# A linear-attention kernel whose first K-weight block is loaded and multiplied as two halves of 256 columns

## The chip, the cores and the metric

One core of one Trainium2 chip runs the whole program. The metric is the device time in microseconds of one execution. A change is judged by the medians of several executions of the kernel before and after it.

The engines are named as the profile names them: PE is TensorE (matmuls and transposes), PEld its weight loads, DVE is VectorE, ACT is ScalarE, POOL is GpSimd, and SPq is the queue of SyncE, which here only issues DMAs.

## The reference: what is computed

The input x has 2048 rows of 1024 bf16 numbers. Branch `a` is a linear attention with 32 heads of 32; branch `b` adds a gated feed-forward result to the single row that a router picks; a sigmoid gate mixes the two.

```python
qkv = x @ wqkv                               # 1024 -> 3 x 1024, split into heads
phi = lambda t: where(t > 0, t + 1, exp(t)) + 1e-6
pq, pk = phi(q), phi(k)
kv = einsum("bhsd,bhse->bhde", pk, v)        # summed over all 2048 rows
z  = einsum("bhsd->bhd", pk)
a  = (pq @ kv) / (pq @ z + 1e-6) @ wo
b  = x + (row argmax(x @ w_r): sigmoid * swiglu(x_sel) @ w_down)
out = g * a + (1 - g) * b                    # g = sigmoid(x . gate_w)
```

## The kernel before

**Tiling.** The 2048 rows are 16 tiles `t` of 128 rows (P = 128). The 1024 input features are 8 chunks `c` (KC = 8). TensorE contracts over partitions, so x must be on chip transposed: `xT[:, c, rows]`. For tiles 4 to 15 a transposing DMA writes `xT` (lines 134 and 135). For tiles 0 to 3 x is loaded as it is (`load_x`, lines 114 to 118), TensorE transposes it, and DVE (tiles 0 to 2) or ACT (tile 3) copies the result out of PSUM: `unit_T`, lines 196 to 206. One `unit_T` is eight 128x128 transposes and one copy of 128x1024.

**K and V.** `wkv` holds the K and V weights, 2048 columns in four blocks `nb` of 512. For a row tile and a block, `kv_mm` (lines 217 to 220) issues eight matmuls of 128x512, one for each chunk, into one PSUM bank. For K (nb 0 and 1), `phi_exp` on ACT takes the exponential and `phi_dve` on DVE two more operations (lines 183 to 191); for V, ACT copies.

**The opening.** The order on SP is written out in lines 126 to 136: row tile 0, the first quarter of the first weight block (`load_w0`: two chunks, 512 columns each), row tile 1, the other three quarters, row tiles 2 and 3 in one DMA, the three other blocks of `wkv`, three transposing DMAs, then the Q weights. The order on PE is written out in lines 253 to 274:

- seven matmuls on zeros (`warm(N_WARM)`), the transposes of tile 0, three more on zeros;
- two chunks of tile 0's K block, the transposes of tile 1, two chunks, one matmul on zeros, the last four chunks;
- four chunks of tile 1's block, the transposes of tile 2, the last four chunks of tile 1;
- the transposes of tile 3, then the blocks of tiles 2 and 3 (lines 273 and 274).

Line 283 then transposes the router weights (`wps` in the profile), and lines 285 to 287 run blocks 1 to 3 of tiles 0 to 3. After that the tiles go on one by one, with Q units and the feed-forward pieces set among them, and the output stage ends the program.

**What fixes the order.** The wrapper `in_order` (lines 68 to 81) ties each instruction of PE, DVE, ACT and SP to the one issued before it on the same engine, as long as `strict[0]` is true; it is so until line 290. Up to there each engine runs its instructions exactly as written. PSUM tiles with the tag "w" share four banks (`ps_work`, line 60): the results of the transposes and those of the matmuls both.

**In the profile.** The recorded line of every wrapped instruction is the wrapper's, L73, so groups are told apart by tile names: `warm_ps` is a matmul on zeros, `pst` a transpose of x, `ps<-wkv,xT` a K or V matmul, `xT<-pst` the copy behind a transpose, `xnat` the loaded row tiles.

Of the kernel before, what the change touches and what calls it, by code (L numbers as in the profile page):

```python
# [12 lines left out]
F32 = mybir.dt.float32  # L13
# [7 lines left out]
P = 128  # L21
S = 2048
D = 1024
F = 3584
NT = S // P
KC = D // P
NG = D // P
EPS = 1e-6
N_WARM = 7
Q_PER_T = {4: 2, 5: 1, 6: 1, 7: 2, 8: 1, 9: 1, 10: 2, 11: 1, 12: 1, 13: 2, 14: 1, 15: 0}  # L30
FFN_PER_T = {6: 8, 7: 0, 8: 8, 9: 0, 10: 8, 11: 0, 12: 8, 13: 1, 14: 7, 15: 7}
FFN_DEPTH = 10
# [4 lines left out]
def kernel(  # L37
# [16 lines left out]
    wqkv_v = A_wqkv.rearrange("(c p) n -> p c n", p=P)  # L54
# [5 lines left out]
    ps_work = ctx.enter_context(tc.tile_pool(name="ps_work", bufs=4, space=PSUM))  # L60
# [7 lines left out]
    def in_order(engine, names):  # L68
        last = [None]

        def wrap(fn):
            def call(*a, **k):
                inst = fn(*a, **k)  # L73
                if last[0] is not None and strict[0]:
                    tc.add_manual_dep(inst.ins, last[0].ins.name, NOSYNC, reason="program order on this engine")
                last[0] = inst
                return inst

            return call

        return SimpleNamespace(**{n: wrap(getattr(engine, n)) for n in names})

    pe = in_order(nc.tensor, ["matmul", "transpose"])
    dve = in_order(nc.vector, ["memset", "tensor_copy", "tensor_scalar", "tensor_scalar_add", "tensor_tensor", "scalar_tensor_tensor",
                               "reciprocal", "max", "max_index", "tensor_reduce", "stream_shuffle"])
    sp = in_order(nc.sync, ["dma_start", "dma_start_transpose"])
# [12 lines left out]
    xT = pa.tile([P, KC, S], BF)  # L99
# [7 lines left out]
    wkv = pw.tile([P, KC, 2 * D], BF)  # L107
# [6 lines left out]
    def load_x(t0, n):  # L114
        xt4 = xin.tile([P, n, D], BF, name=f"xnat{t0}", bufs=1)
        sp.dma_start(out=xt4[:, 0:n, :], in_=x_v[:, t0 : t0 + n, :])
        for i in range(n):
            xnat[t0 + i] = xt4[:, i, :]

    def load_w0(c2):  # L120
        sp.dma_start(out=wkv[:, 2 * c2 : 2 * c2 + 2, 0:512], in_=wqkv_v[:, 2 * c2 : 2 * c2 + 2, D : D + 512])

    def load_wkv(nb):
        sp.dma_start(out=wkv[:, :, 512 * nb : 512 * nb + 512], in_=wqkv_v[:, :, D + 512 * nb : D + 512 * nb + 512])

    load_x(0, 1)
    load_w0(0)
    load_x(1, 1)
    for c2 in range(1, 4):
        load_w0(c2)  # L130
    load_x(2, 2)
    for nb in range(1, 4):
        load_wkv(nb)
    for g4 in range(1, 4):
# [48 lines left out]
    def phi_exp(ps):  # L183
        e0 = tmp.tile([P, 512], F32, tag="phi_e0")
        act.activation(e0[:], ps, ACTF.Exp)
        return e0

    def phi_dve(ps, e0, out_ap):
        e1 = tmp.tile([P, 512], F32, tag="phi_e1")
        dve.tensor_scalar(e1[:], e0[:], 1.0, EPS, op0=ALU.min, op1=ALU.add)  # L190
        dve.scalar_tensor_tensor(out_ap, ps, 0.0, e1[:], op0=ALU.max, op1=ALU.add)
# [4 lines left out]
    def unit_T(t):  # L196
        xt = xnat[t]
        pst = ps_work.tile([P, D], BF, tag="w")
        for c in range(KC):
            pe.transpose(pst[:, c * P : (c + 1) * P], xt[:, c * P : (c + 1) * P], ident[:])  # L200
        dst = xT[:, :, t * P : (t + 1) * P]
        src = pst[:].rearrange("p (c s) -> p c s", c=KC)
        if t < 3:
            dve.tensor_copy(dst, src)
        else:
            act.copy(dst, src)

    pk_t = {}
    vt_t = {}

    def kv_open(t):
        if t not in pk_t:
            pk_t[t] = kvp.tile([P, D], BF, tag="pk", name=f"pk{t}")
            vt_t[t] = kvp.tile([P, NG, 129], BF, tag="vt", name=f"vt{t}")
            nc.gpsimd.memset(vt_t[t][:, :, 128:129], 1.0)  # L215

    def kv_mm(ps, t, nb, c0, c1):
        for c in range(c0, c1):
            pe.matmul(ps[:], lhsT=xT[:, c, t * P : (t + 1) * P], rhs=wkv[:, c, 512 * nb : 512 * nb + 512],
                             start=(c == 0), stop=(c == KC - 1))  # L220

    def kv_evac(ps, t, nb):
        if nb < 2:
            phi_dve(ps[:], phi_exp(ps[:]), pk_t[t][:, 512 * nb : 512 * nb + 512])
        else:
            act.copy(vt_t[t][:, 4 * (nb - 2) : 4 * (nb - 2) + 4, 0:128], ps[:].rearrange("p (g e) -> p g e", g=4))

    def unit_KV(t, nb):
        kv_open(t)
        ps = ps_work.tile([P, 512], F32, tag="w")  # L230
        kv_mm(ps, t, nb, 0, KC)
        kv_evac(ps, t, nb)
# [16 lines left out]
    def warm(n):  # L249
        for _ in range(n):  # L250
            pe.matmul(warm_ps[:], lhsT=warm_sb[:, 0:P], rhs=warm_sb[:], start=True, stop=True)

    warm(N_WARM)
    kv_open(0)
    kv_open(1)
    unit_T(0)
    warm(3)
    ps0 = ps_work.tile([P, 512], F32, tag="w")
    kv_mm(ps0, 0, 0, 0, 2)
    unit_T(1)  # L260
    ps1 = ps_work.tile([P, 512], F32, tag="w")
    kv_mm(ps0, 0, 0, 2, 4)
    warm(1)
    kv_mm(ps0, 0, 0, 4, 8)
    e00 = phi_exp(ps0[:])
    kv_mm(ps1, 1, 0, 0, 4)
    unit_T(2)
    kv_mm(ps1, 1, 0, 4, 8)
    unit_T(3)
    e01 = phi_exp(ps1[:])  # L270
    phi_dve(ps0[:], e00, pk_t[0][:, 0:512])
    phi_dve(ps1[:], e01, pk_t[1][:, 0:512])
    for t in (2, 3):
        unit_KV(t, 0)
    pidx_f = const.tile([P, 4], F32)
    dve.tensor_copy(pidx_f[:], pidx_i[:])
    dve.tensor_scalar(selg[:], pidx_f[:], 0.0, None, op0=ALU.is_equal)
# [14 lines left out]
    for c in range(KC):  # L292
        for j in range(4):
            pe.matmul(rps[32 * j : 32 * j + 32, :], lhsT=wrg_pad[:, c, :], rhs=xT[:, c, 512 * j : 512 * j + 512],
                                  start=(c == 0), stop=(c == KC - 1), tile_position=(0, 32 * j))
# [278 lines left out]
    for t in range(NT):  # L574
# [8 lines left out]
        for c0, cw in cols:  # L583
            ps = ps_work.tile([P, 512], F32, tag="w")
            for g in range(NG):
                pe.matmul(ps[:, 0:cw], lhsT=pq_all[:, g, t * P : (t + 1) * P], rhs=m_sb[:, g, c0 : c0 + cw],
                                 start=(g == 0), stop=(g == NG - 1))
# [41 lines left out]
```

## Time and profile before

| what | us |
|---|---|
| median of 4 runs (lowest to highest) | 266.71 (265.83 to 267.56) |
| the profiled execution, its own time | 266.07 |
| its span, first to last instruction | 264.5 |
| PE busy in it | 255.8 (97%) |
| DVE, ACT, POOL busy | 145.1, 88.3, 49.1 |
| mean granted TensorE clock | 0.998 |

The span is what the profiler records between the first and the last instruction; 1.6 us of the execution's own time lie outside it. Busy times of different engines overlap and do not add up to the span. "Landing" below is the time at which a DMA's completion reaches the semaphore that its readers wait for.

The opening loads in the trace, by the order in which SP issues them (us from the span's start):

| load | issued at | landed at |
|---|---|---|
| x tile 0, 256 KB | 0.98 | 3.69 |
| first block, chunks 0 and 1, 256 KB | 1.44 | 4.50 |
| x tile 1, 256 KB | 1.90 | 5.93 |
| first block, chunks 2 and 3 | 2.43 | 6.79 |
| first block, chunks 4 and 5 | 2.91 | 7.67 |
| first block, chunks 6 and 7 | 3.42 | 8.43 |
| x tiles 2 and 3, 512 KB | 3.93 | 10.03 |
| second block of wkv, 1024 KB | 4.44 | 13.04 |
| fourth block of wkv, 1024 KB | 5.97 | 19.13 |
| the three transposing DMAs | 10.31, 21.98, 26.31 | 24.56, 28.95, 32.78 |
| Q weights, 2048 KB | 30.77 | 39.14 |

### The profile page before, as it was taken

The numbers are of one execution on the slowest core, as the hardware profiler recorded it, in microseconds if no ns is written. First come the engines' busy times: TensorE is split into PE (matmuls) and PEld (weight loads), VectorE is DVE, ScalarE is ACT, GpSimd is POOL, SyncE is SP. The second block draws the span as 40 slices with busy tenths as digits, with TensorE's granted clock in tenths as the row PEclk, the third lists the DMA queues.
The fourth block names the chain that finished last, engine by engine and source line by source line (L and its number), as shares of the span: only waits on it lengthen the run. The fifth ranks groups of instructions, "written<-read, shape, count | busy, mean of one in ns | idle before, by whom it ended". The sixth has DMA issues, their size and how long they took to land.

```text
span 264.5 us, 3982 instructions
## 1 busy us (share of the span) xinstructions
PE 255.8 (97%) x1514; PEld 121.4 (46%) x1541; DVE 145.1 (55%) x280; ACT 88.3 (33%) x137; POOL 49.1 (19%) x101
## 2 busy tenths in 40 slices
PE   7999999999899999999999999999999899999995
PEld 3444454445344444444444455544444344444443
DVE  1385015436184343448523524379999979964443
ACT  1243332323233223323223332233577452333310
POOL 7000001010000000000000000102869219970000
PEclk9999999999999999999999999999999999999999
DMA  6999980009998996039129508094000275454222
GB/s 198 348 311 205 223 306 0 0 10 363 466 406 269 380 364 250 0 105 339 75 85 341 212 0 315 5 308 150 1 4 0 66 227 151 142 189 155 85 79 81
DMA packets 33060, 47.72 MB, mean 180 GB/s; under 512 B 14153, under 2 KB 18641, under 8 KB 32977
## 3 DMA queue, kind: packets, MB, share of 16 engines
q1 hardware_dynamic: 32752, 47.32, 54.1%
q8 instruction: 12, 0.20, 0.3%
q0 software_dynamic: 256, 0.14, 0.2%
q14 instruction: 8, 0.06, 0.1%
q10 hardware_dynamic: 32, 0.00, 0.0%
HBM read 39.85 MB, written 8.39 MB: 182 GB/s over the span
## 4 chain that ended last, share of the span: by engine, by line
PE 64%; DMA 15%; DVE 13%; issue 3%; SPq 3%; ACT 0%; POOLq 0%; DVEq 0%; POOL 0%
PE ps L73 59%; DMA wt<-in_B_w_up_dram 12%; DVE rb L73 4%; DVE pq_all L73 4%; DVE e L73 4%; DMA xnat<-in_A_x_dram 2%; PE kvacc L73 2%; SPq L370 2%; PE yps L73 1%; SPq L73 1%; PE rps L73 1%; DMA xsel<-in_A_x_dram 1%; PE dps L73 1%; PE pst L73 0%; POOLq L331 0%
## 5 line engine op out<-in xcount | busy, mean ns | idle before, releaser
L73 PE MATMUL ps<-wkv,xT 128*128 128x512 bf16 x498 | 114.9, 379 | 1.2 <-DMA wkv<-in_A_wqkv_dram 0.2
L73 PEld LDWEIGHTS <-xT 128*128 128x128 bf16 x512 | 48.7, 98 | 57.2 <-issue 2.5
L73 ACT ACTIVATE e<-ps 128x512 f32<-128x512 f32 x64 | 38.2, 597 | 80.8 <-PE ps L73 76.8
L73 DVE TENSOR_SCALAR e<-e 128x512 f32<-128x512 f32 x64 | 31.4, 492 | 56.2 <-ACT e L73 56.0
L73 PE MATMUL ps<-xT,wq 128*128 128x512 bf16 x248 | 58.1, 379 | 0.4
L73 PE MATMUL ps<-m_sb,pq_all 128*128 128x512 bf16 (+1 forms) x259 | 55.3, 372 | 1.0 <-DVE pq_all L73 0.6
L73 PEld LDWEIGHTS <-pq_all 128*128 128x128 bf16 x264 | 25.7, 98 | 31.3 <-issue 1.8
L543 POOL TENSOR_TENSOR pq_all<-pq_all,rb 128x512 bf16<-128x512 bf16 x32 | 37.2, 1200 | 10.4 <-DVE rb L73 10.4
L73 PEld LDWEIGHTS <-wq 128*128 128x128 bf16 x256 | 24.9, 98 | 30.2 <-issue 0.9
L73 DVE SCALAR_TENSOR_TENSOR ot<-ps,gate,xg 128x512 bf16<-128x512 f32 (+1 forms) x33 | 24.0, 735 | 16.1 <-PE ps L73 16.0
L73 ACT CAST vt<-ps 128x512 bf16<-128x512 f32 x32 | 18.8, 588 | 41.4 <-PE ps L73 41.4
L73 ACT ACTIVATE xg<-xt,omg 128x1024 f32<-128x1024 bf16 x16 | 18.2, 1148 | 25.9 <-DVE ot L73 25.9
L73 DVE STREAM_SHUFFLE rb<-rdp 128x512 f32<-128x512 f32 x32 | 22.8, 744 | 0.0
L73 DVE SCALAR_TENSOR_TENSOR pk<-ps,e 128x512 bf16<-128x512 f32 x32 | 22.1, 690 | 1.1
L73 DVE SCALAR_TENSOR_TENSOR pq_all<-ps,e 128x512 bf16<-128x512 f32 x32 | 21.8, 684 | 0.5
L215 POOL MEMSET vt<- 128x8 bf16 x16 | 1.9, 136 | 106.4 <-PE kvacc L73 106.4
L73 PEld LDWEIGHTS <-pk 128*128 128x128 bf16 x128 | 8.5, 98 | 3.3 <-issue 0.4
L73 PE MATMUL kvacc<-vt,pk 128*128 128x129 bf16 x128 | 9.7, 221 | 0.0
L73 PE MATMUL ps<-wt,xs_pad 128*32 128x512 bf16 x112 | 8.0, 381 | 1.1 <-DMA wt<-in_B_w_gate_dram 0.7
L73 ACT CAST m_sb<-ps 128x512 bf16<-128x512 f32 x16 | 8.6, 591 | 0.0
L73 DVE CAST r_bf<-rps 128x512 bf16<-128x512 f32 x1 | 0.7, 692 | 13.9 <-PE rps L73 13.9
L429 POOL DMA_DIRECT2D xp<-brow x1 | 0.6, 576 | 38.5 <-DVE brow L73 38.5
(99 smaller groups left out, 84.8 us busy)
## 6 DMA issues: line engine op xcount, KB each, us to landing
wt<-in_B_w_down_dram SPq DMA_DIRECT2D x14, 512.0 KB, 6.8
wt<-in_B_w_gate_dram SPq DMA_DIRECT2D x8, 512.0 KB, 8.5
wt<-in_B_w_up_dram SPq DMA_DIRECT2D x8, 512.0 KB, 19.2
xt<-xp SPq DMA_DIRECT2D x16, 256.0 KB, 2.8
out_dram<-ot SPq DMA_DIRECT2D x15, 256.0 KB, 2.0
wkv<-in_A_wqkv_dram SPq DMA_DIRECT2D x3, 1024.0 KB, 10.9
wt<-in_B_w_gate_dram SPq DMA_DIRECT2D x8, 384.0 KB, 5.9
wt<-in_B_w_up_dram SPq DMA_DIRECT2D x8, 384.0 KB, 5.8
```

The lines of the kernel that those rows point to most:

```text
L73: inst = fn(*a, **k)
L215: nc.gpsimd.memset(vt_t[t][:, :, 128:129], 1.0)
L370: ld = nc.sync.dma_start(out=wt[:, 0 : 512 * nr], in_=wv[:, c, c0 : c0 + 512 * nr])
L429: nc.gpsimd.dma_start(out=xp[bass.ds(nonlocal_idx[0], 1), :].rearrange("o (j n) -> (o j) n", j=4), in_=brow[0:128:32, :])
L543: nc.gpsimd.tensor_tensor(sl, sl, rb[:], op=ALU.mult)
```

## The change

The first 512-column block is loaded as two halves of 256 columns: the left half in two DMAs of 256 KB (four chunks each), the right half in one of 512 KB. The rows of x are now loaded one tile at a time. The order on SP becomes: tile 0, left half (chunks 0 to 3), left half (chunks 4 to 7), tile 1, tile 2, right half, tile 3, and then as before.

On PE, tiles 0, 1 and 2 each run their left half as soon as they are transposed, one after the other, and then their right halves, into the other 256 columns of the same three banks. Each eight matmuls of 512 columns become sixteen of 256. Tile 3 keeps its eight of 512. There are three fewer matmuls on zeros: two fewer ahead of tile 0, and one fewer behind its transposes. The exponentials and the DVE operations keep their shapes and follow the right halves.

```diff
-N_WARM = 7
+N_WARM = 5
...
-    def load_w0(c2):
-        sp.dma_start(out=wkv[:, 2 * c2 : 2 * c2 + 2, 0:512], in_=wqkv_v[:, 2 * c2 : 2 * c2 + 2, D : D + 512])
+    def load_w0(c0, c1, n0):
+        sp.dma_start(out=wkv[:, c0:c1, n0 : n0 + 256], in_=wqkv_v[:, c0:c1, D + n0 : D + n0 + 256])
...
     load_x(0, 1)
-    load_w0(0)
+    load_w0(0, 4, 0)
+    load_w0(4, 8, 0)
     load_x(1, 1)
-    for c2 in range(1, 4):
-        load_w0(c2)
-    load_x(2, 2)
+    load_x(2, 1)
+    load_w0(0, 8, 256)
+    load_x(3, 1)
...
+    def kv_half(ps, t, n0):
+        for c in range(KC):
+            pe.matmul(ps[:, n0 : n0 + 256], lhsT=xT[:, c, t * P : (t + 1) * P], rhs=wkv[:, c, n0 : n0 + 256],
+                      start=(c == 0), stop=(c == KC - 1))
+
     warm(N_WARM)
     kv_open(0)
     kv_open(1)
     unit_T(0)
-    warm(3)
-    ps0 = ps_work.tile([P, 512], F32, tag="w")
-    kv_mm(ps0, 0, 0, 0, 2)
+    warm(2)
+    first = [ps_work.tile([P, 512], F32, tag="w", name=f"first{t}") for t in range(3)]
+    kv_half(first[0], 0, 0)
     unit_T(1)
-    ps1 = ps_work.tile([P, 512], F32, tag="w")
-    kv_mm(ps0, 0, 0, 2, 4)
     warm(1)
-    kv_mm(ps0, 0, 0, 4, 8)
-    e00 = phi_exp(ps0[:])
-    kv_mm(ps1, 1, 0, 0, 4)
+    kv_half(first[1], 1, 0)
     unit_T(2)
-    kv_mm(ps1, 1, 0, 4, 8)
+    kv_half(first[2], 2, 0)
+    kv_open(2)
+    kv_half(first[0], 0, 256)
+    es = [phi_exp(first[0][:])]
     unit_T(3)
-    e01 = phi_exp(ps1[:])
-    phi_dve(ps0[:], e00, pk_t[0][:, 0:512])
-    phi_dve(ps1[:], e01, pk_t[1][:, 0:512])
-    for t in (2, 3):
-        unit_KV(t, 0)
+    kv_half(first[1], 1, 256)
+    es.append(phi_exp(first[1][:]))
+    phi_dve(first[0][:], es[0], pk_t[0][:, 0:512])
+    kv_half(first[2], 2, 256)
+    es.append(phi_exp(first[2][:]))
+    phi_dve(first[1][:], es[1], pk_t[1][:, 0:512])
+    phi_dve(first[2][:], es[2], pk_t[2][:, 0:512])
+    unit_KV(3, 0)
```

## The prediction

> **What bounds the kernel now.** I read the page's table of busy times first, then PE's timeline of the opening, then the DMA issues there. The table:
>
> ```profile
> PE 255.8 (97%) x1514; PEld 121.4 (46%) x1541; DVE 145.1 (55%) x280; ACT 88.3 (33%) x137; POOL 49.1 (19%) x101
> ```
>
> TensorE is busy for 255.8 of 264.5 us, so a change pays only if it takes work off PE or closes a gap of PE. From the router transpose `wps` on, PE's later gaps are few (the largest are 0.8, 0.7 and 0.6 us, in the feed-forward pieces and at the start of the output stage), and what ends them follows from PE's own earlier results: the expert weights are issued only after the router's row fetch. A shift of the opening therefore moves the rest of the kernel with it, and I compare the two kernels by one mark: when `wps` starts. PE's timeline up to there (start, duration, engine, line, operation, tiles, count, and in brackets the idle time before it):
>
> ```profile
> 1.43 3.05 PE L73 MATMUL warm_ps<-warm_sb 128*128 128x512 bf16 x7 [1.43 <-DVE warm_sb L73]
> 4.32 0.61 PE L73 MATMUL pst<-ident,xnat 128*128 128x128 bf16 x8
> 4.76 0.81 PE L73 MATMUL warm_ps<-warm_sb 128*128 128x512 bf16 x3
> 5.71 0.60 PE L73 MATMUL ps<-wkv,xT 128*128 128x512 bf16 x2
> 6.15 0.61 PE L73 MATMUL pst<-ident,xnat 128*128 128x128 bf16 x8
> 6.83 0.59 PE L73 MATMUL ps<-wkv,xT 128*128 128x512 bf16 x2
> 7.26 0.38 PE L73 MATMUL warm_ps<-warm_sb 128*128 128x512 bf16 x1
> 7.71 0.59 PE L73 MATMUL ps<-wkv,xT 128*128 128x512 bf16 x2
> 8.48 1.46 PE L73 MATMUL ps<-wkv,xT 128*128 128x512 bf16 x6 [0.17 <-DMA wkv<-in_A_wqkv_dram]
> 10.08 0.62 PE L73 MATMUL pst<-ident,xnat 128*128 128x128 bf16 x8
> 10.54 1.03 PE L73 MATMUL ps<-wkv,xT 128*128 128x512 bf16 x3
> 11.40 0.61 PE L73 MATMUL pst<-ident,xnat 128*128 128x128 bf16 x8
> 11.85 3.62 PE L73 MATMUL ps<-wkv,xT 128*128 128x512 bf16 x16
> 15.39 0.18 PE L73 MATMUL wps<-ident,wrg_rows 16*128 16x16 bf16 x1
> ```
>
> A row's duration includes the drain of its last matmul, so I take start-to-start times: 0.216 us for a matmul of 512 columns, 0.056 for a transpose. The mark needs 32 matmuls (6.91) and 32 transposes (1.79), 8.70 us of work. From 4.32 to 15.39 are 11.08 us, so 2.38 us are lost: to the first copy, to the quarters of the weights as they land (6.79, 7.67, 8.43), and to tiles 2 and 3, which land at 10.03. That is all that a change of the opening can win.
>
> What hides the copies is to be seen here too. Behind each transpose comes this on DVE:
>
> ```profile
> 4.96 0.69 DVE L73 COPY xT<-pst 128x1024 bf16<-128x1024 bf16 x1 [3.59 <-PE pst L73]
> 6.80 0.69 DVE L73 COPY xT<-pst 128x1024 bf16<-128x1024 bf16 x1 [1.15 <-PE pst L73]
> 10.73 0.69 DVE L73 COPY xT<-pst 128x1024 bf16<-128x1024 bf16 x1 [3.24 <-PE pst L73]
> ```
>
> From the first transpose of a tile to the first matmul that reads its copy are 1.395 us (4.316 to 5.711): 0.447 of transposes, 0.95 of drain, copy and hand-over. Behind tile 1's transposes PE runs six matmuls of tile 0; behind tile 2's, four of tile 1 and tile 3's transposes. Only tile 0's copy stands bare.
>
> **The change step by step.**
>
> *Half-width matmuls: nothing.* The output stage has the form:
>
> ```profile
> L73 PE MATMUL ps<-m_sb,pq_all 128*128 128x256 bf16 x16 | 1.9, 273 | 0.0
> ```
>
> They start 0.109 us apart, half of 0.216, with the doubled weight loads hidden (98 ns each, beside the matmul before). Sixteen halves cost what eight whole ones do: a `kv_half` is 0.872 us.
>
> *Two fewer matmuls ahead of tile 0: 0.34 us won.* At the start the matmuls on zeros are 0.427 us apart, and from about 4.23 on PE runs at 0.216: the granted clock doubles there. Five of them are through at 3.54, so tile 0's transposes start when x lands (3.69), at 3.73. They run at the slow spacing (0.107) until 4.23, then at 0.056: issued by 4.42, drained at 4.59, copied by 5.31; the first half matmul at 5.37 in place of 5.71. The matmuls on zeros that remain lie in the waits behind transposes.
>
> *The loads.* SP still issues each in some 0.47 us, well ahead of the data; the weights now come in runs of 512 bytes. The trace's DMA records give 18 ns for a packet of 256 bytes, 46 for 1 KB, 84 for 2 KB; on the line through them 512 bytes take 27 (an estimate). On 16 DMA engines a left half of 512 packets is 0.86 us against 0.74 for an old quarter of 256, and a row tile of 128 packets 0.67. I shift the measured landings by these differences, place by place: the first left half at 4.50 + 0.13 = 4.63; the second stands where tile 1 stood, 5.93 + 0.13 + 0.19 = 6.25; tile 1 where the second quarter stood, 6.79 + 0.32 - 0.07 = 7.04; tile 2 by 7.9, the right half by 9.9, tile 3 by 10.5, the second block by 13.6. PE asks for the last four at 9.3, 11.6, 12.5 and 16.6, so they wait for nobody. The transposing DMAs move by at most 0.5 us; the last of them (32.78) is first read by the router at 36.3, and the Q weights (39.14) are first needed near 47. Hidden.
>
> *The new order on PE.* Left half of tile 0: four matmuls at 5.37, then a wait for the second left half, four more from 6.29 to 6.73. Tile 1's transposes are next, and its rows land at 7.04: start 7.08. And now each left half stands directly behind its own tile's transposes, with at most one matmul on zeros between. PE runs in the written order, so the 0.95 us of drain, copy and hand-over stand bare for tiles 1 and 2. From tile 1's transposes on:
>
> - transposes to first matmul 1.395, left half of tile 1 0.872
> - transposes of tile 2 to first matmul 1.395, left half of tile 2 0.872
> - right half of tile 0 0.872, transposes of tile 3 0.447, right halves of tiles 1 and 2 1.744
> - tile 3's whole block 1.727, hand-over to `wps` 0.096
>
> Sum 9.42; the mark is at 7.08 + 9.42 = 16.50 against 15.39: **1.11 us later**. Against the 2.38 us lost before, PE now loses, from 3.73 on, 0.95 behind tile 0, 0.49 and 0.35 for DMAs, twice 0.95 behind tiles 1 and 2, 0.2 for slow transposes and 0.1 ahead of `wps`.
>
> *PSUM and the tail.* Three tiles hold three of the four banks, so all transposes go through one. Tile 3's block needs that bank (ACT's copy, done near 14.30) or tile 0's (DVE, near 14.47); PE asks at 14.70. It fits by 0.2 us, and PE's next requests are 1.7 us apart.
>
> [...]
>
> **The sum** against the profiled execution's 266.07 is 267.2. That run lies 0.64 below the median of the runs shown, 266.71; on the median the forecast is **267.8 us**, 0.4% longer. Half a per cent (1.33 us) is about what a measurement of this kernel can tell from no change.
>
> Bounds of the unknown packet: if 512 bytes took half of a 1 KB packet, tile 1 would land at 6.73 and the shift be 0.8; the other bound is the first rival. With some scatter of landings I give the forecast's own case 267.4 to 268.2.
>
> **The rivals.**
>
> *The DMA engines are paid by the packet (15%).* If a packet of 512 bytes takes the 46 ns of one of 1 KB, each left half takes 1.47 us, and tile 1 lands at 6.79 + 0.74 + 0.80 - 0.07 = 8.26: shift 2.3, 269.0. For it: between 4 and 8 us the DMAs move some 300 GB/s at a busy share near 1.0, below the 358 after 10 us, so something other than bytes costs there. Against: 256 bytes take 18 ns, less than half of 46.
>
> *The fast clock comes late (17%).* It came after 2.8 us of nearly unbroken matmuls on zeros. Now they end at 3.54, 0.7 us sooner, with a gap of 0.2 us and transposes behind them. If PE stays at the slow spacing up to tile 1's transposes, tile 0's copy ends 0.2 us later, both parts of its left half take 0.85, tile 1's transposes start at 7.26 and take 0.85, and its first matmul comes at 9.07, not 8.48: 0.6 more, 1.7 in all, 268.4. [...] The trace shows one rise, and no kernel with fewer matmuls ahead of it.
>
> *Not slower: the landings of ordinary executions (15%).* The old order stands or falls with tiles 2 and 3, for which PE waits until 10.03; the new one has over a microsecond of slack for every load after tile 1. If in unprofiled runs that landing is later and tile 1's is not, only the old kernel pays. From 11.1 on the two are equal. The 0.64 us between the profiled run and the median could be this: then 267.2, or no difference. Against: nothing in the trace sets the sixth load apart from the fourth.
>
> *The order is not what it seems (3%).* If PE did not keep to the written order, the copies of tiles 1 and 2 would be covered, 1.9 us less: 265.9. The wrapper's order holds in every row above.
>
> The rest of the chance, 50%, is the forecast's. Its upper edge, with the first two rivals, makes slower by over 0.5% 40%; within 0.5% 57%; faster 3%. The range, 266.4 to 269.0, runs from the third rival to the first.
>
> **What will show it.** Right: tile 1's transposes near 7.1, gaps of nearly a microsecond on PE before the left halves of tiles 1 and 2, half matmuls 0.109 us apart, `wps` near 16.5, and nothing changed behind it but the shift. Wrong: tile 1's transposes right behind tile 0's left half at 6.3 (the landings), or after 8 (packets); matmuls 0.427 apart after 4.3 (clock); a wait before tile 3's block (PSUM); a `wps` before 15.4.

## The result and the profile after

The changed kernel takes **267.71 us** (median of 49 runs, 266.49 to 271.47), the kernel before 266.95 (75 runs, 265.62 to 268.8). The ratio is 1.003 with a 95% interval of 1.002 to 1.0039: the medians differ by 0.76 us, and the interval is 0.5 to 1.0 us. The forecast was 1.11 us slower, 267.8. So the direction is right and the size somewhat too large: 1.11 us lies just above the interval. That 267.8 is so near to 267.71 is in part luck, since the forecast started from the median of four runs, 266.71, which is 0.24 us below that of the 75.

The profiled execution took 266.82 us, its span is 265.3 (before: 266.07 and 264.5). TensorE's busy time, in the page's first table of the changed kernel, fell by 0.5 us while the span grew by 0.8:

```profile
PE 255.3 (96%) x1535; PEld 123.3 (46%) x1562; DVE 145.0 (55%) x280; ACT 88.2 (33%) x137; POOL 49.0 (18%) x101
```

PE's timeline of the opening after the change (columns as before: start, duration, engine, line, operation, tiles, count, idle time ahead):

```profile
1.43 2.31 PE L73 MATMUL warm_ps<-warm_sb 128*128 128x512 bf16 x5 [1.43 <-DVE warm_sb L73]
3.74 0.92 PE L73 MATMUL pst<-ident,xnat 128*128 128x128 bf16 x8
4.50 0.59 PE L73 MATMUL warm_ps<-warm_sb 128*128 128x512 bf16 x2
5.45 0.61 PE L73 MATMUL first<-wkv,xT 128*128 128x256 bf16 x4 [0.35 <-DVE xT L73]
6.96 0.60 PE L73 MATMUL first<-wkv,xT 128*128 128x256 bf16 x4 [0.90 <-DMA wkv<-in_A_wqkv_dram]
7.65 0.62 PE L73 MATMUL pst<-ident,xnat 128*128 128x128 bf16 x8
8.11 0.38 PE L73 MATMUL warm_ps<-warm_sb 128*128 128x512 bf16 x1
9.06 1.05 PE L73 MATMUL first<-wkv,xT 128*128 128x256 bf16 x8 [0.57 <-DVE xT L73]
9.94 0.61 PE L73 MATMUL pst<-ident,xnat 128*128 128x128 bf16 x8
11.34 1.92 PE L73 MATMUL first<-wkv,xT 128*128 128x256 bf16 x16 [0.79 <-DVE xT L73]
13.10 0.61 PE L73 MATMUL pst<-ident,xnat 128*128 128x128 bf16 x8
13.54 1.91 PE L73 MATMUL first<-wkv,xT 128*128 128x256 bf16 x16
15.29 1.89 PE L73 MATMUL ps<-wkv,xT 128*128 128x512 bf16 x7
17.11 0.18 PE L73 MATMUL wps<-ident,wrg_rows 16*128 16x16 bf16 x1
```

The reader sees each step of the forecast in it. Five matmuls on zeros, tile 0's transposes at 3.74, a first half matmul at 5.45. Then 0.90 us of waiting for the second left half, then the pattern that repeats: transposes, a bare gap that ends with "DVE xT", a left half. From 13.54 on PE is dense: sixteen half matmuls up to 15.29 are 0.109 us each, and tile 3's block follows at once, with no wait for its PSUM bank. The mark `wps` stands at 17.11, 1.72 us later than before (15.39).

The copies behind the transposes (DVE's timeline of the changed kernel) take what they took; they come at other times:

```profile
4.70 0.69 DVE L73 COPY xT<-pst 128x1024 bf16<-128x1024 bf16 x1 [3.33 <-PE pst L73]
8.31 0.69 DVE L73 COPY xT<-pst 128x1024 bf16<-128x1024 bf16 x1 [2.92 <-PE pst L73]
10.59 0.69 DVE L73 COPY xT<-pst 128x1024 bf16<-128x1024 bf16 x1 [1.59 <-PE pst L73]
```

And PE's own list of waits (who waits for whom: us in total, times, the longest) now holds two rows on `first` that the kernel before does not have:

```profile
PE first L73 <- DVE xT L73: 1.7, 3, 0.8
...
PE first L73 <- DMA wkv<-in_A_wqkv_dram: 0.9, 1, 0.9
```

Where PE's later work stands in the two profiled executions, by when its first instruction of a kind starts:

| PE reaches | before | after | difference |
|---|---|---|---|
| the mark `wps` | 15.39 | 17.11 | 1.72 |
| the router's selected row (`xs_ps`) | 59.63 | 61.35 | 1.72 |
| the first feed-forward piece | 70.02 | 72.17 | 2.15 |
| the row tile behind the first pieces | 76.17 | 77.47 | 1.31 |
| the row tile behind the second pieces | 98.69 | 99.36 | 0.67 |
| the end of the span | 264.52 | 265.27 | 0.75 |

The shift is not rigid, as the prediction had taken it to be. It grows by 0.43 at the router and shrinks by 1.47 over the first two groups of feed-forward pieces. So there are two questions: is the opening longer for the reason given, and what gives back half of it later?

### The profile page after: what moved, and what is told of

It reads as the page before. It is cut to its first block, busy times and chain, and to the rows that moved or that the text cites. A ratio compares the mean times of both kernels' runs of the same rounds, so it can differ in the third digit from the quotient of the medians.

```text
span 265.3 us, 4026 instructions
## 1 busy us (share of the span) xinstructions
PE 255.3 (96%) x1535; PEld 123.3 (46%) x1562; DVE 145.0 (55%) x280; ACT 88.2 (33%) x137; POOL 49.0 (18%) x101
## 4 chain that ended last, share of the span: by engine, by line
PE 82%; DVE 11%; DMA 3%; issue 2%; SPq 1%; ACT 0%; POOL 0%; DVEq 0%
PE ps L73 73%; DVE rb L73 4%; DVE e L73 3%; PE kvacc L73 3%; DVE pq_all L73 2%; DMA xnat<-in_A_x_dram 2%; PE first L73 2%; DMA rdp<-rd 1%; PE yps L73 1%; PE rps L73 1%; PE pst L73 1%; PE dps L73 1%; DVE xT L73 1%; SPq L73 1%; PE gl_ps L73 0%
## 5 line engine op out<-in xcount | busy, mean ns | idle before, releaser
L73 PE MATMUL ps<-wkv,xT 128*128 128x512 bf16 x474 | 108.9, 379 | 0.7
L73 PEld LDWEIGHTS <-xT 128*128 128x128 bf16 x536 | 50.9, 98 | 58.2 <-issue 2.8
L73 ACT ACTIVATE e<-ps 128x512 f32<-128x512 f32 x61 | 36.4, 597 | 74.1 <-PE ps L73 70.7
L73 DVE SCALAR_TENSOR_TENSOR pk<-ps,e 128x512 bf16<-128x512 f32 x29 | 20.0, 690 | 1.0
L73 PE MATMUL first<-wkv,xT 128*128 128x256 bf16 x48 | 6.1, 273 | 2.6 <-DVE xT L73 1.7
```

## The experiments

**A pure delay** (`delay8`): the old kernel with eight more matmuls on zeros right ahead of the mark, 1.73 us of nothing else.

```diff
     for t in (2, 3):
         unit_KV(t, 0)
+    warm(8)
```

> The kernel before with eight matmuls on zeros put right ahead of the router transpose: a pure delay of the opening by 8 x 0.216 = 1.73 us, as large as the shift of 1.72 us that the changed kernel's trace shows at that mark. Theory A (part of any delay of the opening is won back where TensorE waits for the expert weights, at the first feed-forward pieces): the mark is 1.7 us later, the waits of 0.8 and 0.6 us at 71 and 94 us are gone or smaller, and the time rises by only 0.7 to 1.1 us. Theory B (a delay passes through whole, and the opening of the changed kernel's profiled execution was slow by chance): the time rises by 1.7 us, and waits of about that size are still there.

Measured: 269.42 us (6 runs) against 266.93, ratio 1.0086 (1.0059 to 1.0113): 2.3 us, from 1.6 to 3.0. In its profiled run the eight stand here:

```profile
16.35 1.89 PE L73 MATMUL warm_ps<-warm_sb 128*128 128x512 bf16 x8
18.29 0.16 PE L73 MATMUL wps<-ident,wrg_rows 16*128 16x16 bf16 x1
```

A delay of PE ahead of the mark is paid, no part of it is seen to be swallowed: Theory A's 0.7 to 1.1 us lie outside the interval, and PE still waits 1.3 us for the gate weights in this profile. What the changed kernel gets back must come from something else in it than from its being late. (In this run the mark lies 1.17 us later than the delay explains: tile 1 landed at 7.47, not at 5.93.)

**The copies covered** (`cover`): the changed kernel with tile 2's transposes ahead of tile 1's left half, as the old order had something between a tile's transposes and its matmuls. Loads and half matmuls stay.

```diff
-    first = [ps_work.tile([P, 512], F32, tag="w", name=f"first{t}") for t in range(3)]
+    first = [ps_work.tile([P, 512], F32, tag="w", name=f"first{t}") for t in range(2)]
     kv_half(first[0], 0, 0)
     unit_T(1)
-    warm(1)
-    kv_half(first[1], 1, 0)
     unit_T(2)
+    kv_half(first[1], 1, 0)
+    first.append(ps_work.tile([P, 512], F32, tag="w", name="first2"))
     kv_half(first[2], 2, 0)
```

> The changed kernel with tile 2's transposes ahead of the left half of tile 1 (third PSUM tile taken later, the matmul on zeros behind tile 1 left out). If the bare copies of tiles 1 and 2 are what the change costs: tile 2's copy runs under the left half of tile 1, the router transpose starts near 15.7 us in place of 17.1, and the time is 0.6 to 1.4 us under the changed kernel's, within 0.3 us of the kernel before. If late weights are the cost instead: the mark stays near 17 and the time at the changed kernel's.

Measured: 266.71 us (12 runs) against 266.93 of the old kernel on that chip, ratio 0.9983 (0.9965 to 1.0002). PE's timeline of it:

```profile
6.91 1.37 PE L73 MATMUL pst<-ident,xnat 128*128 128x128 bf16 x16
8.31 2.79 PE L73 MATMUL first<-wkv,xT 128*128 128x256 bf16 x24
10.94 0.61 PE L73 MATMUL pst<-ident,xnat 128*128 128x128 bf16 x8
...
14.96 0.18 PE L73 MATMUL wps<-ident,wrg_rows 16*128 16x16 bf16 x1
```

Sixteen transposes in one row, and then 24 half matmuls without a gap. From tile 1's landing (6.86, which is why the mark comes before the expected 15.7) to the mark are 8.10 us; in the changed kernel they are 9.50. The 1.40 us are the gap behind tile 2's transposes (0.95), which is gone, and the part of the gap behind tile 1's (0.45) that tile 2's transposes now fill; some 0.5 us of that one stay bare. With that the whole loss of the changed kernel is gone: `cover` stands 0.22 us below the old kernel, where the changed one stands 0.76 above it, and its interval takes in no difference. Its loads are the changed kernel's, runs of 512 bytes and all, so these loads by themselves do not make a kernel slower than the old one.

It does not win, though its mark is 0.43 us ahead of the old kernel's. In the profiled run it is 0.93 us ahead of it behind the expert weights too, and ends 0.33 behind. On PE the 1.26 us go between 186 and 204 us, at the hand-overs from matmuls on `wo` to the next group: 0.74 us from start to start at 187 us and 0.48 at each of 190 and 192, where a matmul is 0.216. Between the kernels before and after this stage makes 0.08 us of difference. The trace has the wait behind it on DVE, over which the chain of work that ended last runs in this stage: `rdp`, four loads of 32 KB, comes late. That chain has 4.54 us of `rdp` in it in `cover` and none in the old kernel. DVE's line, first in `cover`, then in the old kernel (idle for 0.13 us there, too short to be listed):

```profile
184.00 0.01 DVE L73 LOAD_MASK_SELECT rb<-rdp  x1 [1.40 <-DMA rdp<-rd]
```

```profile
183.65 0.01 DVE L73 LOAD_MASK_SELECT rb<-rdp  x1
```

The first `rdp` load is issued 0.94 us earlier in `cover` (178.25 and 179.19), the last one lands 0.35 us later (183.81 and 183.47). The 2 MB load of `wo` is still under way when they are issued (in the old kernel it lands at 180.7, 9.7 us behind its issue, and the last `rdp` load is issued at 180.20), and it was issued only 0.18 us earlier (170.83 and 171.01). So the lead that PE had gained ended at a DMA that was hardly earlier. Whether the unprofiled runs lose it in the same place is not shown.

**The row tiles alone** (`split_x`): the old kernel with rows 256 to 511 loaded as two DMAs.

```diff
-    load_x(2, 2)
+    load_x(2, 1)
+    load_x(3, 1)
```

> The kernel before with row tiles 2 and 3 loaded by two DMAs: nothing else changed. Tile 2's transposes waited until 10.03 for both tiles; alone, tile 2 should land near 9.3, before TensorE asks at 9.77: mark 0.3 us earlier. Theory B: 0.3 us faster. Theory A: 0 to 0.2 us faster, since an earlier opening waits longer for the expert weights.

Measured: 266.99 (12 runs) against 266.93, ratio 1.0004 (0.9985 to 1.0023). Tile 2's transposes start at 9.82 in place of 10.08, the mark comes at 15.12, and the time does not show it; the interval, 0.4 us less to 0.6 more, takes in both theories.

**Runs of 512 bytes in the old order** (`runs512`): every quarter of the first block in two DMAs of 256 columns.

```diff
-        sp.dma_start(out=wkv[:, 2 * c2 : 2 * c2 + 2, 0:512], in_=wqkv_v[:, 2 * c2 : 2 * c2 + 2, D : D + 512])
+        for n0 in (0, 256):
+            sp.dma_start(out=wkv[:, 2 * c2 : 2 * c2 + 2, n0 : n0 + 256], in_=wqkv_v[:, 2 * c2 : 2 * c2 + 2, D + n0 : D + n0 + 256])
```

> The kernel before with each quarter of the first block loaded by two DMAs of 256 columns, so that all of it comes in runs of 512 bytes; the order on TensorE is the old one. It prices the 512-byte runs alone. If a packet of 512 bytes takes 27 ns, as the changed kernel's trace says: the eight loads cost 0.5 us more in sum, tiles 2 and 3 land some 0.4 to 0.6 us later, and the time rises by 0.3 to 0.6 us. If 512 bytes run at the full rate: no change. If DMA engines were paid by the packet: 2.9 us more.

Measured: 268.68 (8 runs, 266.76 to 270.98) against 266.89, ratio 1.0089 (1.0054 to 1.0123): 2.4 us, from 1.4 to 3.3, where 0.3 to 0.6 were expected for packets of 27 ns. The profiled run is the fastest of the eight, so its rows (mark at 16.17, PE waiting for quarters at 7.54 and 9.49) do not show where the others lose their two microseconds. Besides the shorter runs it has four more DMAs, and SP issued its twelfth and thirteenth only after the landings at 6.63 and 7.04; which of the two costs the time is not told apart by this run. What it does settle is the packet: 27 ns for 512 bytes, in this kernel's records as in those of the changed one.

**Tile 1 first** (`split_around`): the changed kernel with tile 1's load ahead of the second left half, and PE's order to match, so that tile 0's left half is split around tile 1's transposes and tile 1's copy lies beside matmuls.

```diff
     load_w0(0, 4, 0)
-    load_w0(4, 8, 0)
     load_x(1, 1)
+    load_w0(4, 8, 0)
...
-    first = [ps_work.tile([P, 512], F32, tag="w", name=f"first{t}") for t in range(3)]
-    kv_half(first[0], 0, 0)
+    first = [ps_work.tile([P, 512], F32, tag="w", name=f"first{t}") for t in range(2)]
+    kv_half(first[0], 0, 0, 0, 4)
     unit_T(1)
-    warm(1)
-    kv_half(first[1], 1, 0)
+    kv_half(first[0], 0, 0, 4, 8)
     unit_T(2)
+    kv_half(first[1], 1, 0)
+    first.append(ps_work.tile([P, 512], F32, tag="w", name="first2"))
     kv_half(first[2], 2, 0)
```

(The last two arguments of `kv_half` are the first chunk and the one behind the last.)

> The changed kernel with row tile 1 loaded ahead of the second left half, and on TensorE: half of tile 0's left half, tile 1's transposes, the other half, tile 2's transposes, then the left halves of tiles 1 and 2. All copies of tiles 1 and 2 are covered, and the load that stands third is no longer one that all the rest waits for. Theory (bare copies are the cost, loads the rest): mark 14.5 to 15.0 where the third load lands near 6, about 15.5 where it lands near 7; time 0.2 to 0.6 us under the kernel before. If the copies are not what costs: no better than the changed kernel.

Measured: 266.96 (12 runs) against 266.89, ratio 0.9998 (0.9979 to 1.0017). The third load, now tile 1, lands at 7.15, and the mark comes at 15.94. The mark is 0.4 us later than expected for such a landing, and the 0.2 to 0.6 us under the old kernel are not there. Like `cover` it takes the changed kernel's loss away and wins nothing against the old one, and like `cover` its DVE waits for `rdp`, 1.32 us.

**The same kernels again** (`again`, `again2`: the changed one; `old_again`: the old one), one profile each.

> The changed kernel once more, unchanged, for a second profile. Theory A: mark again 1.3 to 1.8 us later than before's 15.39, no wait of over 0.3 us at the first feed-forward pieces. Theory B: the second left half lands near 6.3, not 6.9, mark near 16.5, and the waits at the feed-forward pieces differ from those of the first profile.

> The changed kernel once more. Theory: the router transpose starts 9.5 us after row tile 1 lands, as in both profiles so far (7.61 to 17.11, 7.87 to 17.38), so near 16.4 where the second left half lands near 6.0 and near 17.2 where it lands near 7.

> The kernel before, unchanged, for a further profile of its opening. Theory (the third load lands near 6.0 in some executions and near 7.2 in others, whatever it carries, and both kernels pay for it alike): the mark is either near 15.4 or near 16.5, and follows the landing of row tile 1. Rival (late landings belong to the changed kernel's 512-byte loads): near 15.4.

Measured, in us from the span's start, with two other kernels that have the old loads or nearly so:

| run | third load landed | tile 1 landed | fast clock from | mark | span |
|---|---|---|---|---|---|
| before | 5.93 | 5.93 | 4.23 | 15.39 | 264.5 |
| old_again | 6.67 | 6.67 | 5.09 | 15.92 | 264.9 |
| split_x | 5.96 | 5.96 | 6.60 | 15.12 | 264.1 |
| delay8 | 7.47 | 7.47 | 4.71 | 16.56 and 1.73 | 267.8 |
| after | 6.91 | 7.61 | 4.41 | 17.11 | 265.3 |
| again | 7.19 | 7.87 | 5.16 | 17.38 | 266.2 |
| again2 | 6.33 | 7.02 | 6.04 | 16.52 | 265.2 |

In the three executions of the changed kernel the mark follows tile 1's landing by 9.50, 9.51 and 9.50 us; the forecast had 9.46. `again2` is the prediction's own case, landings and all:

```profile
7.06 0.62 PE L73 MATMUL pst<-ident,xnat 128*128 128x128 bf16 x8
...
8.47 1.05 PE L73 MATMUL first<-wkv,xT 128*128 128x256 bf16 x8 [0.57 <-DVE xT L73]
...
16.52 0.18 PE L73 MATMUL wps<-ident,wrg_rows 16*128 16x16 bf16 x1
```

So the changed kernel's opening is understood, and its scatter is that of one landing; `again`, with the latest one, has a mark that neither of its two theories had. The third load lands anywhere from 5.93 to 7.47, whatever it carries and in both kernels: not near one of two values, as was expected of `old_again`. The old kernel's mark follows it less closely, 9.46 us behind the landing in `before`, 9.25 in `old_again` and 9.09 in `delay8` (without its eight matmuls). The records of the first 6 us hold packets that take many times longer than their like (512 bytes 1.07 us at 4.25 in the changed kernel, 2 KB 1.25 us at 4.40 in `delay8`, where 27 and 84 ns are usual later). That these packets are what makes the load late was not tested.

**What gives time back.** PE's list of waits has two rows on the expert weights in the old kernel, and none in the changed one:

```profile
PE ps L73 <- DMA wt<-in_B_w_gate_dram: 0.7, 1, 0.7
...
PE ps L73 <- DMA wt<-in_B_w_up_dram: 0.5, 1, 0.5
```

In the six profiles of the old order (before, old_again, split_x, delay8, runs512, and plain_old below) these rows come to 0.5 to 1.3 us; in the three of the changed kernel none is listed. In the profiled pair they are the whole of the 1.47 us: from the first piece to the row tile behind it the changed kernel takes 0.84 us less, and from that row tile to the one behind the second pieces 0.64. Two things differ. First, the 0.43 us that the changed kernel loses at the router: the gate weights are already on their way then (issued 42.81 us behind the mark, as before), so pieces that are asked for 0.4 us later wait 0.4 less. Where that loss arises is to be seen on DVE, first in the old and then in the changed kernel:

```profile
60.11 0.19 DVE L73 CAST xs_pad<-xs_ps 128x8 bf16<-128x8 f32 x1 [4.25 <-PE xs_ps L73]
```

```profile
62.25 0.19 DVE L73 CAST xs_pad<-xs_ps 128x8 bf16<-128x8 f32 x1 [4.67 <-PE xs_ps L73]
```

PE's selected row is done at 60.00 and at 61.72; the copy of it starts 0.11 us later in the one and 0.53 in the other, with DVE idle and no wait left that the trace shows. All five profiles with half matmuls have it (0.52 or 0.53), none of the eight without them (0.11, from the end of PE's last instruction there). DVE's stream is three instructions longer in the new one; that this is why is not shown.

Second, SP's issue of the eight gate weights, of which three take 0.43 us each in the old kernel and three in the changed one. First in the old, then in the changed kernel (start, time of the whole group, engine queue, line, operation, tiles, count):

```profile
58.19 5.48 SPq L370 DMA_DIRECT2D wt<-in_B_w_gate_dram  x8
```

```profile
59.92 3.86 SPq L378 DMA_DIRECT2D wt<-in_B_w_gate_dram  x8
```

One of the eight takes 1.76 us in the old kernel; the longest in the changed one is 0.51. The records show a 16 KB packet of instructions, one of twelve on the queue q8, at 60.9 in the old kernel, inside that stretch, and at 57.0 in the changed one, ahead of it. I take it for TensorE's, whose stream is 42 rows longer there (1535 matmuls and 1562 weight loads on the page, 1514 and 1541 before). Theory C, formed at this point: the longer stream moves the packet out of the weights' way, and that is the time given back. Its rival: the two have nothing to do with each other.

**The length of TensorE's stream** (`plain_old`, `plain_pad42`, `plain_pad14`): the old kernel with the three transposing loads made plain (it leaves the transposition of those rows out, so only its time and trace are of use), and the same with its warm matmuls cut into 28 of 128 columns or 14 of 256, which take the same time on PE.

```diff
-    warm(N_WARM)
+    for _ in range(28):
+        pe.matmul(warm_ps[:, 0:128], lhsT=warm_sb[:, 0:P], rhs=warm_sb[:, 0:128], start=True, stop=True)
```

> The kernel before, with the three transposing loads of rows 512 to 2047 replaced by plain loads of the same bytes: the transposition of those rows is left out in this kernel and in the two beside it, which differ from it only in the number of warm matmuls. It is the base for both. Theory C (the changed kernel wins part of its delay back at the first expert weights, because its 42 more TensorE instructions move TensorE's instruction packet from about 60 us to about 56 us, ahead of the expert-weight stream): here the packet comes near 60 us, one issue of an expert weight takes 1.1 to 2.1 us, and the first expert pieces wait 0.9 us or more. Rival (the packet has nothing to do with it): no statement on the packet, waits of any size.

> As plain_old, with the seven warm matmuls of 512 columns replaced by 28 of 128 columns, the same TensorE time in more instructions (an instruction stream longer by 42 rows, as in the changed kernel). Theory C: TensorE's instruction packet comes near 56 us, no issue of an expert weight takes over 0.7 us, the first expert pieces wait under 0.5 us, and the run is 0.4 to 1.0 us faster than plain_old. Rival: the waits at the first expert pieces stay at 0.9 us or more and the time is that of plain_old within 0.3 us.

> As plain_old, with the seven warm matmuls replaced by 14 of 256 columns (a stream longer by 14 rows). Theory C: the packet comes near 59 us, still inside the expert-weight stream, and issue times, waits and time are those of plain_old within 0.3 us. Rival: the same as for plain_pad42.

| kernel | median of 12 runs | packet at | eight issues, longest one | waits for gate and up weights |
|---|---|---|---|---|
| plain_old | 266.42 | 59.4 | 5.22, 1.89 | 0.6 and none |
| plain_pad42 | 266.18 | 56.2 | 3.74, 0.47 | 0.3 and 0.3 |
| plain_pad14 | 267.41 | 59.0 | 6.08, 1.47 | 0.9 and 0.7 |

The last one's rows, issues and then waits:

```profile
58.72 6.08 SPq L372 DMA_DIRECT2D wt<-in_B_w_gate_dram  x8
```

```profile
PE ps L73 <- DMA wt<-in_B_w_gate_dram: 0.9, 1, 0.9
PE ps L73 <- DMA wt<-in_B_w_up_dram: 0.7, 1, 0.7
```

Half of Theory C holds: the packet moves with the length of the stream as expected (59.4, 59.0, 56.2), and where it comes ahead of the weights no issue is slow. The other half does not. The waits of `plain_old` are 0.6 us where 0.9 or more was expected; those of `plain_pad42` are 0.6 as well, not under 0.5; and a gain is not shown: 0.24 us less, with an interval from 0.86 less to 0.80 more. And `plain_pad14`, expected within 0.3 us of `plain_old`, is 0.99 us slower (0.38 to 1.82); its profiled run has 1.0 us more of the two waits. The rival, which took the three for equal, did not expect that either: the kernel with fourteen more rows in TensorE's stream (seven matmuls and their weight loads), and the same time of PE's work, takes a microsecond longer, and the one with 42 more does not. Why is not shown. (The intervals are resampled from the 12 and 12 runs.)

Over all thirteen profiles the first half stands: in the seven where the packet comes between 59.0 and 61.9 us, one issue takes 1.07 to 2.11 us; in the six where it comes between 54.8 and 57.4, none takes over 0.66. The two waits come to 0.5 to 1.6 us in the seven, on average 0.97. In the six they come to 0.0 to 0.6; with the 0.4 that the router's delay covers in five of them, on average 0.53.

What stays open is how the 1.47 us given back in the profiled pair split up. The router's 0.43 us account for that much. The slow issues go with some 0.4 more on average, by rows that scatter more widely than that, and the medians of `plain_pad42` and `plain_pad14` don't bear it out. The pair is also on the high side. From the mark to the row tile behind the second pieces the three profiles of the changed kernel take 82.39 us on average, and four with the old opening (before, old_again, delay8, plain_old) 83.14: 0.75 us are given back there, the router's loss already taken off. DVE's wait for `rdp` takes 0.2 of it again (0.46 on average in the three, 0.25 in the four), and from the mark to the end 0.54 are left (248.56 and 249.10), where the profiled pair has 0.96. I leave the meeting of packet and weights as a trait that both kernels' profiles show, and no cause that is proved.

## Why the prediction was right, point by point

**TensorE is the bound, and the mark tells it: half right.** PE's time ahead of the mark is paid, as `delay8` shows. But the step "a shift of the opening therefore moves the rest of the kernel with it" failed. The prediction had looked for later gaps whose end follows from PE's own results, and had found that all do. It did not ask whether the way there stays the same in a kernel with another instruction stream. The runs showed 0.43 us more at the router and 1.47 less at the expert weights in the profiled pair, and 0.54 less on average over seven profiles.

**The bare copies: right, to 0.04 us.** "Sum 9.42" behind tile 1's transposes; from the landing of tile 1 the forecast was 9.46 and the runs gave 9.50. Of the "twice 0.95", `cover` takes 1.40 us away and leaves 0.5 bare.

**Half matmuls at nothing: right.** 0.109 us each, weight loads hidden.

**Two fewer matmuls on zeros: the 0.34 us are there and buy nothing.** The first half matmul comes at 5.45 (forecast 5.37, before 5.71), and PE then waits 0.90 us for the second left half. The forecast's chain had started at tile 1's landing, so no error came of it.

**The loads: the packet right, the landings those of one execution.** Packets of 512 bytes take 27 ns, the estimate to the nanosecond; the first rival, 46 ns, falls. But the landings were carried over from one execution, whose third load is the earliest of all in the table. Forecast for tile 1: 7.04. Measured: 7.61, 7.87, 7.02, and the mark on average at 17.00, 0.50 later than forecast. The old opening is later on average, too: 15.39, 15.92, 16.56 (`delay8` without its eight matmuls) and 15.44 (plain_old) make 15.83, 0.44 later than the one profile. That is a shift of 1.17 us, near the 1.11, because the lateness stands on both sides. Without `delay8` it would be 1.42: with marks that scatter by 0.9 us in the changed kernel and 1.2 in the old opening, three and four profiles give the shift to a few tenths only.

**The clock: the rival falls.** With five matmuls on zeros the granted clock rises at 4.41, 5.16 and 6.04; with seven at 4.23, 5.09, 4.71 and 6.60. In `cover` and `split_around`, with five, it rises at 6.11 and 6.10, so a somewhat later rise with fewer matmuls is not excluded; but it comes ahead of tile 1's transposes in all five, and the changed kernel's mark stands 9.50 us behind tile 1's landing whether it comes at 4.41 or at 6.04. In `again2` it rose late, at 6.04, while tile 0's half matmuls ran (their row of eight takes 1.14 us there, those behind it 1.05), and its mark is the earliest of the three, since PE waits for tile 1 in any case.

**Landings of ordinary executions: its reason falls.** Late landings are common to both kernels, and the row tiles alone (`split_x`) change nothing. The result lies between this rival and the forecast, but for another reason.

**The sum.** In the opening about 1.2 in the profiles, near the 1.11; behind it about 0.5 given back, which the prediction had not counted; together 0.6, and 0.76 in the medians (0.5 to 1.0). So the forecast shift is 0.35 us too large, by these profiles for the step on the rigid shift, and the base is 0.24 too low. The two partly cancel in the 267.8.

The packet times also settle what the halves cost per byte. Packets of 512 bytes take 27 ns, which on 16 engines is 303 GB/s; 1 KB takes 46 ns, 356 GB/s; 2 KB 84 ns, 390 GB/s. The landings agree: the right half, 512 KB in packets of 512 bytes, lands 1.73 us behind tile 2's rows in the changed kernel (8.34 to 10.07), which is 302 GB/s. So the halves do cost more per byte than the quarters, which came in packets of 1 KB.

## What to carry to other kernels

Cutting a load so that work can start on its first half only pays if the engine has other work to lay beside the latencies that the new order bares; here two copies of 0.69 us stood bare where the old order had matmuls of the other tile beside them, and putting the next tile's transposes there took the loss away. It did not make a gain: PE's lead was gone again where a later stage waited for a DMA, so a shift that is read at one mark has to be followed to the end. A forecast from landings needs more than one execution of them: one load's landing scattered by 1.5 us, which is twice the effect that was to be measured. And below a microsecond two kernels with the same work can differ for reasons far from the change: the same warm matmuls cut into 14 pieces made a kernel 0.99 us slower, and cut into 28 they did not.

## What the runs showed of the hardware

- A load of 256 KB, the third issued, lands between 5.93 and 7.47 us, in one kernel and across kernels, and single packets of 1.07 and 1.25 us stand in the records ahead of the late ones.
- The record of the granted clock at full speed begins between 4.1 us (`plain_old`) and 6.6 us (`split_x`), in six profiles with seven matmuls on zeros ahead of it at 4.82 on average, in five with five at 5.56; so few don't tell the two apart. In `before` it begins at 4.23, and the matmuls on zeros are 0.427 us apart up to there and 0.216 behind it. It lasts 259.41 us in `before` and 262.83 in `after`.
- Packets of 16 KB on the instruction queue q8, twelve in `before` and in `after`, take 0.88 to 1.45 us of a DMA engine there, at times that follow the number of TensorE's instructions: 42 more rows moved the one near 60 us to 56 (59.4 in `plain_old`, 56.2 in `plain_pad42`). That they cost time is not shown: a kernel with 14 more rows was 0.99 us slower (0.38 to 1.82), one with 42 more was not (0.86 less to 0.80 more).
- DVE started a copy 0.42 us later than else with its input long ready, at one and the same place in all five profiles with half matmuls and in none of the eight others; the cause is not known.
- Four loads of 32 KB, issued while a load of 2 MB is under way, landed all four 3.19 us after the last one's issue in `delay8` and 4.54 in `cover`. DVE waited 1.40 us for them in `cover` and 1.32 in `split_around`.
